# Nineteen differences per head for queries and keys, and the sums of key features times values taken head by head

## The chip, the cores and the metric

The kernel runs on one core of one Trainium2 chip. The metric is the time of one execution on the device in microseconds (us). Before the change the median of three runs is 1411.07 us (1410.63 to 1412.09).

Five engines work side by side, each through its own queue of instructions: TensorE (PE; its weight loads are a row of their own, PEld), VectorE (DVE), ScalarE (ACT), GpSimd (POOL) and SyncE (SP), which here issues the DMAs.

## What is computed

Two layers, each a linear attention with a learned feature map followed by a dense block, on 2048 rows of 640 numbers. Cut to what the change touches:

```
qkv = layernorm(x) @ wqkv                     # 32 heads of 20
pq, pk = q @ w_phi[h], k @ w_phi[h]           # per head, 20 by 20
phi = concat(softmax(p), softmax(-p))         # 40 features per head
kv  = sum over rows of phi_k * v              # per head 40 x 20
z   = sum over rows of phi_k                  # per head 40
o   = (phi_q @ kv) / (phi_q @ z + 1e-6)
x   = x + o @ wo
x   = x + mish(layernorm(x) @ w1 + b1) @ w2
```

A softmax over 20 numbers does not change when one and the same number is taken from all 20. So `p[d] - p[0]` serves as well as `p[d]`, and its first entry is always 0.

## The kernel before, in words

**Rows and blocks.** The 2048 rows are 16 tiles of 128 rows; two tiles are a block (8 blocks). A product in almost full precision is made of three matmuls on `fp32r` numbers, with both sides split into a high and a low part: high times high, high times low, low times high. So one projection of one tile to 640 columns is 2 halves of 320 columns x 5 parts of the inner dimension x 3 = 30 matmuls (`project`, `project_half`, line 344). Where the tables say `128x320`, that is the output of one of them. A plain `f32` matmul (transposes, the sums below, the averages) appears in the profile as two MATMUL instructions.

**The feature weights** are folded once, in layer 0: `fold_phi` (line 237) multiplies the weights of queries and of keys by the block-diagonal `phi_bd` (6 heads of 20 columns to a block, 120 columns to a matmul), splits the product into high and low part (ACT line 242, DVE line 243), and `spill_qk_weights` stores them in `wp_d` for layer 1.

**attend_first** goes over the 8 blocks. Per tile it projects keys, values and queries (`project`), and makes features of keys and queries (`features`): ACT copies the 640 numbers out of PSUM to every second group of 20 of a tile `e` of 1280 columns; DVE finds each head's maximum and minimum (368); DVE or POOL (369) and DVE (371) take them off; ACT takes the exponential of all 1280 (374, through the helper at 116); DVE sums each group (377) and inverts (378); POOL multiplies (379). Values go to a tile `v` of 21 columns per head, the last one 1, so that `z` comes out with `kv`. Then `keys` accumulates over the rows (line 414): for each of 11 groups of three heads (the last of two) one f32 matmul with the 63 columns of `v` as weights and the 120 features of the group as moving columns. Even groups write PSUM partitions 0 to 63, odd groups 64 to 127, of the tiles `kva` (groups 0 to 7) and `kvz` (8 to 10). Query features are turned by DVE (423) and stored in HBM (`e_d`).

**The passage.** All products of a group, also those of one head's features with another head's values, are in the sums. `finish_kv` clears the foreign ones by a multiplication with `head_mask` (three DVE products, 535), turns the result on PE (six transposes, 543) and copies it to `kvb` (ACT, DVE 547 and 548). The last query projection is spread around it: `rest()` issues its first half ahead of the last sums, and three fifths and two fifths of its second half before and after the transposes.

**attend_second** reads the query features back, multiplies them by `kvb` (`average`, line 571), divides (DVE 580 to 584) and applies `wo` (line 344 again). **dense** follows (lines 679 and 721).

**Order.** In `attend_second` and in the start of layer 0 the order of PE and SP (at the start of SP alone) is the one written down (`manual_schedule`); elsewhere a scheduler puts the instructions of each engine in order when the program is built. Every ACT instruction made by `act` comes after the one made before it. PSUM has two tiles `mm` of two banks each and four tiles `one` of one bank each.

Of the kernel before, what the change touches and what calls it, by code (L numbers as in the profile page):

```python
# [29 lines left out]
HC = D // 2  # L30
EW = 2 * D
# [7 lines left out]
E_CAP = 65536.0  # L39


@with_exitstack
def kernel(
# [48 lines left out]
    mask = const.tile([P, 120], F32, name="mask")  # L92

    kvb = const.tile([120, GP, P], F32, name="kvb")
# [4 lines left out]
    wp_d = dram.tile([2, 2, KD, P, D], F32, name="wp_d")  # L99
# [75 lines left out]
    def load_q_weights():  # L175
        ws = [r2_pair(k) for k in range(KD)]
        for k in range(KD):
            for s in range(2):
                nc.sync.dma_start(ws[k][s].bitcast(F32), wp_d[0, s, k])
        return ws  # L180

    def load_k_weights(kv_ws):
        for k in range(KD):
            for s in range(2):
                nc.sync.dma_start(kv_ws[k][s][:, :D].bitcast(F32), wp_d[1, s, k])

    def spill_qk_weights(kv_ws, q_ws):
        for k in range(KD):
            for s in range(2):
                nc.sync.dma_start(wp_d[1, s, k], kv_ws[k][s][:, :D].bitcast(F32))  # L190
                nc.sync.dma_start(wp_d[0, s, k], q_ws[k][s].bitcast(F32))
# [34 lines left out]

    def fold_phi(ws, bd, raw):

        pss = {}
        for k, c in ((0, 0), (1, 0), (2, 0), (3, 0), (0, 1), (1, 1), (2, 1), (3, 1), (4, 0), (4, 1)):  # L230
# [4 lines left out]
            for t in range(3 * c, 3 * c + 3):  # L235
                r, rows = raw[t]
                nc.tensor.matmul(ps[:, (t % 3) * 120:(t % 3) * 120 + rows],
                                 r[:rows, k * P:(k + 1) * P], bd[:rows, t, :rows],
                                 start=True, stop=True)
            n0, n1 = (0, 360) if c == 0 else (360, D)  # L240
# [88 lines left out]
    def project(xts, t, ws, col, ps=None):  # L329
# [4 lines left out]
        for c in range(2):  # L334
            project_half(ps[c], xts, t, ws, col, c)
        return ps

    def project_half(ps, xts, t, ws, col, c, ks=range(KD)):
        sl = slice(t * P, (t + 1) * P)
        cs = slice(col + c * HC, col + (c + 1) * HC)  # L340
        for k in ks:
            h, l, wh, wl = xts.hs[k], xts.ls[k], ws[k][0][:, cs], ws[k][1][:, cs]
            for n, (a, r) in enumerate(((h, wh), (h, wl), (l, wh))):
                nc.tensor.matmul(ps[:, :HC], a[:, sl], r, start=(k == 0 and n == 0),  # L344
                                 stop=(k == KD - 1 and n == 2))

    def both(ps):

        return ps[2][:, :, :HC]


# [3 lines left out]
    def features(ps, e, pool_sub):  # L355
# [3 lines left out]
        ec = e.rearrange("p (c h s d) -> p s c h d", c=2, s=2, d=DH)[:, 1]  # L359
        if len(ps) > 2:  # L360
            act(ec, both(ps).rearrange("p c (h d) -> p c h d", d=DH), AF.Copy)
        else:
            for c in range(2):
                act(ec[:, c], ps[c][:, :HC].rearrange("p (h d) -> p h d", d=DH), AF.Copy)
# [22 lines left out]
    def attend_first(layer, x_src, first):  # L387
# [18 lines left out]
        def keys(xts, i, v):  # L406
            e = big_tile()
            yield from features(project(xts, i % BT, kv_ws, 0), e, False)
            yield
            for g in range(G):  # L410
                p, n = divmod(g, 2)
                w, m = (120, 64) if g < 10 else (80, 42)
                acc, c = (kva, 120 * p) if p < 4 else (kvz, 120 * (p - 4))
                nc.tensor.matmul(acc[64 * n:64 * n + m, c:c + w], v[:, GW * g:GW * g + m],  # L414
                                 e[:, 120 * g:120 * g + w],
                                 start=(i == 0 and p in (0, 4)), stop=(i == NT - 1),
                                 skip_group_check=True)

        def queries(xts, i, ps=None):
            e = query_tile(i)  # L420
            yield from features(project(xts, i % BT, q_ws, 0) if ps is None else ps, e, True)
# [23 lines left out]
        if first is None:  # L445
            with tc.manual_schedule(engines={mybir.EngineType.SP}):
                bd = big_tile()[:120, :720].rearrange("p (t c) -> p t c", t=6)
                nc.sync.dma_start(bd[:, :3], phi_bd[:, :3])
                raw = load_raw(0, range(3))
                xt = fetch_normed(0)  # L450
                nc.sync.dma_start(bd[:, 3:], phi_bd[:, 3:])
                raw += load_raw(0, range(3, 6))
                nxt = normed(0, xt).all()
# [4 lines left out]
            nc.sync.dma_start(mask, head_mask)  # L458
# [3 lines left out]
        for b in range(NB):  # L462
# [9 lines left out]
            for n, (kind, t) in enumerate(order):  # L472
# [5 lines left out]
                if b == 0 and n == 3:  # L478
                    if layer == 0:
                        fold_phi(kv_ws, bd, raw)  # L480
                    kva, kvz = one_tile(), one_tile()
# [19 lines left out]
        def rest():  # L501

            ps = [one_tile(), one_tile()]
            project_half(ps[0], xts, 1, q_ws, 0, 0)
# [3 lines left out]
            project_half(ps[1], xts, 1, q_ws, 0, 1, range(3))  # L508
            yield
            project_half(ps[1], xts, 1, q_ws, 0, 1, range(3, KD))  # L510
# [6 lines left out]
        return kva, kvz, o_ws, loaded, rest()  # L517
# [12 lines left out]
    def finish_kv(kva, kvz, mask):  # L530
# [349 lines left out]
```

## Time and profile before

| | before |
|---|---|
| median of 3 runs | 1411.07 us |
| profiled execution, first to last instruction | 1410.6 us |
| PE busy | 1391.5 us (99%), 11528 matmuls |
| DVE busy | 1077.9 us (76%) |
| ACT busy | 583.6 us (41%) |
| POOL busy | 460.6 us (33%) |
| attend_first, layer 0 | up to about 274 us |
| attend_first, layer 1 | about 783 to 959 us |

The profile is of one execution. The span runs from its first to its last instruction; the table's 1410.6 us is the profiled execution's own time as the profile has it, and the median of the runs lies 0.5 us above. Matmuls are pipelined: one matmul's busy time is longer than the distance to the start of the next, so what a matmul costs is read from the distance between starts, not from its busy time. A group's row gives line, engine, operation, output and inputs, shapes, count, busy time, mean duration and the idle time ahead of it. In the chain of waits a piece is a stretch of equal instructions with its start and length.

### The profile page before, as it was taken

The numbers are of one execution on the slowest core, as the hardware profiler recorded it, in microseconds if no ns is written. First come the engines' busy times: TensorE is split into PE (matmuls) and PEld (weight loads), VectorE is DVE, ScalarE is ACT, GpSimd is POOL, SyncE is SP. The second block draws the span as 40 slices with busy tenths as digits, with TensorE's granted clock in tenths as the row PEclk, the third lists the DMA queues.
The fourth block names the chain that finished last, engine by engine and source line by source line (L and its number), as shares of the span: only waits on it lengthen the run. The fifth ranks groups of instructions, "written<-read, shape, count | busy, mean of one in ns | idle before, by whom it ended". The sixth has DMA issues, their size and how long they took to land. (4 is left out here: it accounts for less than half of the span.)

```text
span 1410.6 us, 28124 instructions
## 1 busy us (share of the span) xinstructions
PE 1391.5 (99%) x11528; PEld 1369.5 (97%) x11528; DVE 1077.9 (76%) x1810; ACT 583.6 (41%) x973; POOL 460.6 (33%) x344
## 2 busy tenths in 40 slices
PE   7999999999999999999999999999999999999998
PEld 7999999999999999999999999999999999999998
DVE  4798877686688877788769887878767766767765
ACT  4444343321355554455454333332234444444443
POOL 1354444343442221222234443443434211111112
PEclk9999999999999999999999999999999999999999
DMA  8533422789633423343374333357966212333200
GB/s 315 169 78 57 75 38 39 198 231 298 220 100 94 101 77 63 98 113 94 105 270 87 73 65 67 49 113 225 293 229 206 56 31 83 94 94 94 65 30 20
DMA packets 350035, 169.57 MB, mean 120 GB/s; under 512 B 286866, under 2 KB 323458, under 8 KB 349906
## 3 DMA queue, kind: packets, MB, share of 16 engines
q1 hardware_dynamic: 349906, 167.78, 44.1%
q8 instruction: 90, 1.47, 0.4%
q14 instruction: 39, 0.32, 0.1%
HBM read 104.82 MB, written 62.91 MB: 119 GB/s over the span
## 5 line engine op out<-in xcount | busy, mean ns | idle before, releaser
L721 PE MATMUL mm<-r2h,ol 128*128 128x320 f32 x1280 | 305.5, 310 | 1.4 <-ACT ol L704 0.8
L705 POOL TENSOR_TENSOR ol<-big,ol 128x512 fp32r<-128x512 f32 (+1 forms) x98 | 130.0, 1327 | 457.4 <-ACT ol L704 386.8
L679 PE MATMUL one<-xtl,r1h 128*128 128x256 f32 x960 | 268.6, 280 | 2.0 <-DVE xtl L286 2.0
L679 PE MATMUL one<-xth,r1l 128*128 128x256 f32 x960 | 268.0, 279 | 0.0
L679 PE MATMUL one<-xth,r1h 128*128 128x256 f32 x960 | 266.5, 279 | 0.0
L721 PEld LDWEIGHTS mm<-r2h,ol 128*128 128x128 f32 x1280 | 219.1, 188 | 3.1 <-POOL ol L705 1.8
L721 PE MATMUL mm<-r2l,ol 128*128 128x320 f32 x640 | 197.3, 309 | 0.0
L344 PE MATMUL mm<-r1h,xth 128*128 128x320 f32 x600 | 188.3, 314 | 0.0
L344 PE MATMUL mm<-r1h,xtl 128*128 128x320 f32 x600 | 185.7, 310 | 0.7 <-DVE xtl L286 0.7
L344 PE MATMUL mm<-r1l,xth 128*128 128x320 f32 x600 | 185.6, 309 | 0.0
L679 PEld LDWEIGHTS one<-xtl,r1h 128*128 128x128 f32 x960 | 180.4, 188 | 2.7 <-DVE xtl L286 2.5
L679 PEld LDWEIGHTS one<-xth,r1l 128*128 128x128 f32 x960 | 180.4, 188 | 0.0
L679 PEld LDWEIGHTS one<-xth,r1h 128*128 128x128 f32 x960 | 179.9, 188 | 0.0
L344 PE MATMUL mm<-r2h,xth 128*128 128x320 f32 x460 | 144.4, 314 | 0.0
L694 DVE TENSOR_SCALAR big<-big 128x512 f32<-128x512 f32 (+1 forms) x98 | 55.8, 570 | 113.4 <-ACT big L692 111.3
L344 PE MATMUL mm<-r2h,xtl 128*128 128x320 f32 x460 | 142.4, 310 | 0.0
L344 PE MATMUL mm<-r2l,xth 128*128 128x320 f32 x460 | 142.3, 309 | 0.0
L379 POOL TENSOR_TENSOR r<-r,r 128x1280 f32<-128x1280 f32 x32 | 75.7, 2367 | 144.5 <-DVE r L378 138.9
L692 ACT ACTIVATE big<-one,b1s 128x256 f32<-128x256 f32 x192 | 80.8, 469 | 96.0 <-PE one L679 93.8
L721 PEld LDWEIGHTS mm<-r2l,ol 128*128 128x128 f32 x640 | 120.2, 188 | 0.0
L696 ACT ACTIVATE big<-big,two 128x512 f32<-128x512 f32 (+1 forms) x98 | 70.1, 715 | 118.7 <-DVE big L695 116.2
L704 ACT ACTIVATE ol<-big 128x512 fp32r<-128x512 f32 (+1 forms) x98 | 61.0, 622 | 133.6 <-DVE big L703 133.3
(128 smaller groups left out, 3088.2 us busy)
## 6 DMA issues: line engine op xcount, KB each, us to landing
e_d<-r SPq DMA_DIRECT2D x128, 160.0 KB, 4.0
big<-e_d SPq DMA_DIRECT2D x32, 640.0 KB, 7.2
x_d<-xt SPq DMA_DIRECT2D x23, 640.0 KB, 4.1
xt<-x_d SPq DMA_DIRECT2D x22, 640.0 KB, 5.4
n_d<-xn SPq DMA_DIRECT2D x176, 80.0 KB, 2.1
xt<-in_x SPq DMA_DIRECT2D x16, 640.0 KB, 6.7
xn<-x_d SPq DMA_DIRECT2D x28, 320.0 KB, 4.3
v<-n_d SPq DMA_DIRECT2D x30, 256.0 KB, 3.1
```

The costliest lines, as they stand in the source:

```text
L344: nc.tensor.matmul(ps[:, :HC], a[:, sl], r, start=(k == 0 and n == 0), stop=(k == KD - 1 and n == 2))
L379: nc.gpsimd.tensor_tensor(eg, eg, r.unsqueeze(2).to_broadcast([P, 2 * H, DH]), op=ALU.mult)
L679: nc.tensor.matmul(ph[:, j, :], l, r, start=(n == 0), stop=(n == 3 * KD - 1))
L692: exps[0] = nc.scalar.activation(part(ta, 0)[:, j - js.start], ph[:, j, :], AF.Exp, bias=b1s[:, 2 * pr + j:2 * pr + j + 1]).ins
L694: nc.vector.tensor_scalar_min(e, e, E_CAP)
L696: nc.scalar.activation(r, n, AF.Ln, bias=two)
L704: nc.scalar.activation(ah[:, js], n, AF.Copy)
L705: nc.gpsimd.tensor_tensor(al[:, js], n, ah[:, js].bitcast(F32), op=ALU.subtract)
L721: nc.tensor.matmul(pys[t][:, c, :HC], l[:, j, sl], r, start=(f == 0 and n == 0), stop=(f == KF - 1 and n == 2))
```

## The change

It has two parts, and what follows from them.

**Differences.** At the start of layer 0 a new function `differences` takes the first column of each head from its other 19 in `bd`, the block-diagonal feature weights (two DVE instructions). `fold_phi` uses the 19 differences alone, so the folded weights of queries and keys are 608 columns wide in place of 640, and a projection's half is 304 columns in place of 320. Values and `wo` keep 320. `features` writes the 19 numbers behind a zero, which an added ACT instruction sets for all 32 heads of each tile. All later steps see 20 numbers per head, as before.

**Sums head by head.** `keys` issues 32 f32 matmuls per tile, one for each head, with 21 columns of `v` as weights and 40 moving columns. Four successive ones write four different quarters of 32 PSUM partitions (`HEAD_ORDER`, `head_place`). All sums fit one PSUM tile, and `kvz` is gone.

**The passage.** `finish_kv` has one clearing of a 360-column tile on POOL, four copies out of PSUM (one for each quarter, in turn on ACT and DVE), three transposes, and four DVE products with a mask that spread each head's block into `kvb`. The mask is loaded as 120 x 3 numbers. `average` reads `kvb` by group and not by pairs of groups.

```diff
+DF = DH - 1
+FC = H * DF // 2
+FW = H * DF
+HEAD_ORDER = [3 * (4 * n + q) + j for n in range(3) for j in range(3) for q in range(4) if 3 * (4 * n + q) + j < H]
...
-    mask = const.tile([P, 120], F32, name="mask")
-    kvb = const.tile([120, GP, P], F32, name="kvb")
+    mask = const.tile([120, 3], F32, name="mask")
+    kvb = const.tile([120, GP, 2, 64], F32, name="kvb").rearrange("f p q c -> f (p q) c")
...
+    def differences(bd, ts):
+        part = bd[:, ts].rearrange("p t (h d) -> p (t h) d", d=DH)
+        nc.vector.tensor_tensor(part[:, :, 1:], part[:, :, 1:],
+                                part[:, :, :1].to_broadcast([120, 18, DF]), op=ALU.subtract)
...
-                nc.tensor.matmul(ps[:, (t % 3) * 120:(t % 3) * 120 + rows],
-                                 r[:rows, k * P:(k + 1) * P], bd[:rows, t, :rows],
+                n, c0 = rows // DH, (t % 3) * 6 * DF
+                nc.tensor.matmul(ps[:, c0:c0 + n * DF].rearrange("p (h d) -> p h d", d=DF),
+                                 r[:rows, k * P:(k + 1) * P],
+                                 bd[:rows, t].rearrange("p (h d) -> p h d", d=DH)[:, :n, 1:],
...
-    def project_half(ps, xts, t, ws, col, c, ks=range(KD)):
+    def project_half(ps, xts, t, ws, col, c, ks=range(KD), w=HC):
-        cs = slice(col + c * HC, col + (c + 1) * HC)
+        cs = slice(col + c * w, col + (c + 1) * w)
-                nc.tensor.matmul(ps[:, :HC], a[:, sl], r, start=(k == 0 and n == 0),
+                nc.tensor.matmul(ps[:, :w], a[:, sl], r, start=(k == 0 and n == 0),
...
+    def head_place(h):
+        g, j = divmod(h, 3)
+        return g % 4, 2 * DH * (3 * (g // 4) + j)
...
+        act(eh[:, 1, :, 0], ident[:, :H], AF.Copy, scale=0.0)
-            act(ec, both(ps).rearrange("p c (h d) -> p c h d", d=DH), AF.Copy)
+            act(ec[..., 1:], both(ps, FC).rearrange("p c (h d) -> p c h d", d=DF), AF.Copy)
...
-            for g in range(G):
-                p, n = divmod(g, 2)
-                w, m = (120, 64) if g < 10 else (80, 42)
-                acc, c = (kva, 120 * p) if p < 4 else (kvz, 120 * (p - 4))
-                nc.tensor.matmul(acc[64 * n:64 * n + m, c:c + w], v[:, GW * g:GW * g + m],
-                                 e[:, 120 * g:120 * g + w],
+            for h in HEAD_ORDER:
+                q, c = head_place(h)
+                nc.tensor.matmul(kva[32 * q:32 * q + DH + 1, c:c + 2 * DH], v[:, (DH + 1) * h:(DH + 1) * (h + 1)],
+                                 e[:, 2 * DH * h:2 * DH * (h + 1)], start=(i == 0 and c == 0), stop=(i == NT - 1),
...
-    def finish_kv(kva, kvz, mask):
+    def finish_kv(kva):
+        acc = row_tile()
+        nc.gpsimd.memset(acc[:, :360], 0.0)
+        yield
+        for q, n in enumerate((9, 9, 8, 6)):
+            part = (slice(32 * q, 32 * q + DH + 1), slice(0, 40 * n))
+            if q % 2:
+                nc.vector.tensor_copy(acc[part], kva[part])
+            else:
+                act(acc[part], kva[part], AF.Copy)
+        yield
+        ps = one_tile().rearrange("p (n q c) -> p n q c", n=4, c=32)
+        for n in range(3):
+            nc.tensor.transpose(ps[:120, n], acc[:, 120 * n:120 * (n + 1)], ident)
+        for n, q, r, w in ((0, 4, 120, 3), (1, 4, 120, 3), (2, 2, 120, 3), (2, 1, 80, 2)):
...
+            nc.vector.tensor_tensor(
+                kvb[:r, g:g + q, :(DH + 1) * w].rearrange("f q (j c) -> f q j c", j=w),
+                ps[:r, n, q0:q0 + q, :DH + 1].unsqueeze(2).to_broadcast([r, q, w, DH + 1]),
+                mask[:r, :w].unsqueeze(1).unsqueeze(3).to_broadcast([r, q, w, DH + 1]), op=ALU.mult)
...
-                        kvb[:n, g // 2, 64 * (g % 2):64 * (g % 2) + w], start=True, stop=True)
+                        kvb[:n, g, :w], start=True, stop=True)
```

More of the change, by code (lines that the diff above doesn't have):

```diff
@@ L420, in queries @@
             e = query_tile(i)
[L421 removed]
+            yield from features(project(xts, i % BT, q_ws, 0, w=FC) if ps is None else ps, e, True)
             nc.vector.transpose(e, e)
@@ L609, in attend_second @@
         with tc.manual_schedule(engines={mybir.EngineType.PE, mybir.EngineType.SP}):
-            kv = finish_kv(kva, kvz, mask)
+            kv = finish_kv(kva)
+            next(kv)
             next(rest)
```

59 lines of the change are left out of this document (24 added, 35 removed).

## The prediction

> **What bounds the kernel now.** First the head of the page, then its slices: PE is busy for 99% of the span at the full clock, and DVE is the next engine.
>
> ```profile
> span 1410.6 us, 28124 instructions
> PE 1391.5 (99%) x11528; PEld 1369.5 (97%) x11528; DVE 1077.9 (76%) x1810; ACT 583.6 (41%) x973; POOL 460.6 (33%) x344
> PEclk9999999999999999999999999999999999999999
> ```
>
> A busy PE isn't a bound by itself, so next the chain of waits, in order of time, in the middle of layer 1's attend_first:
>
> ```profile
> 839.51 13.40 PE mm L344 x90
> 852.91 1.31 PE one L414 x22
> 854.22 13.40 PE mm L344 x90
> ```
>
> Nothing but PE is in it. One tile takes 854.22 - 839.51 = 14.71 us: 90 matmuls of the three projections and 22 instructions of the sums (11 f32 matmuls, two instructions each). So here the matmuls' own price decides, and both parts of the change touch just these two groups.
>
> What does a matmul cost by its width? The same chain in the dense block, where two widths follow each other:
>
> ```profile
> 1160.06 3.50 PE one L679 x30
> 1163.56 3.53 PE mm L721 x24
> ```
>
> 256 columns take 3.50/30 = 116.7 ns from start to start, 320 columns 3.53/24 = 147.1 ns. The price goes with the columns (0.456 and 0.460 ns each).
>
> **The change part by part.**
>
> *Projections.* Keys and queries have 2 layers x 16 tiles x 60 = 1920 matmuls. 304 columns at 0.46 ns cost 139.7 ns, so each saves 7.35 ns (7.6 by the slope between the two rows, 6.7 if a sixteenth of it did not follow the width). 30 matmuls per layer stand at the passage, treated below; the other 1860 save **13.7 us** (12.4 to 14.1).
>
> *Sums.* The timeline has a burst for one tile in layer 0 (195.45), the burst for two tiles at layer 1's passage (953.57), and, for the price of full width, the f32 matmuls of fold_phi:
>
> ```profile
> 195.21 0.31 PE L344 MATMUL mm<-r2h,xtl 128*128 128x320 f32 x1
> 195.45 1.38 PE L414 MATMUL one<-big,v 128*64 128x120 f32 x22
> 196.76 0.66 PE L280 MATMUL one<-ident,xn 128*128 128x128 f32 x4
> ...
> 953.57 2.54 PE L414 MATMUL one<-big,v 128*64 128x120 f32 x44
> 956.04 0.41 PE L344 MATMUL one<-r2h,xth 128*128 128x320 f32 x1
> ...
> 36.34 0.82 PE L237 MATMUL mm<-big,raw 120*128 120x120 f32 x6
> 37.01 0.83 PE L237 MATMUL one<-big,raw 120*128 120x120 f32 x6
> ```
>
> One tile: 196.76 - 195.45 = 1.31 us. Two tiles: 956.04 - 953.57 = 2.47 us. So the second costs 1.16 us: that is the stream of 22 instructions, 53 ns each, and 0.15 us is paid once per burst (with 0.09 us ahead of it: 0.24 from the last matmul's start to the burst's, where 0.147 is usual). At full output width 120 columns cost 0.67/6 = 112 ns. 53 is about half: the two halves of 64 output partitions work side by side.
>
> The new stream has 64 instructions of 40 columns, on four quarters. By the full-width price one costs 112/3 = 37 ns in its quarter. The fullest quarter has 9 heads, 18 instructions: 0.67 us if the four go side by side as the two do now. I take 0.68, since the weight loads get shorter too:
>
> ```profile
> L414 PEld LDWEIGHTS one<-big,v 128*64 128x64 f32 x640 | 32.7, 136 | 6.7 <-issue 5.6 <-POOL big L379 1.1
> L414 PEld LDWEIGHTS one<-big,v 128*42 128x42 f32 x64 | 7.1, 118 | 0.0
> ```
>
> The fixed part stays, since the burst's count and place do. But the number of instructions goes from 22 to 64 (and as many loads), and no row shows four quarters. The nearest rows in width are those of the averages, 42 and 63 columns on two halves:
>
> ```profile
> 959.35 1.38 PE L571 MATMUL mm<-kvb,big 120*64 120x63 f32 x40
> 960.57 0.27 PE L571 MATMUL mm<-kvb,ol 80*64 80x42 f32 x4
> 960.66 1.36 PE L571 MATMUL mm<-kvb,big 120*64 120x63 f32 x40
> ```
>
> 63 columns: (960.57 - 959.35)/40 = 30.5 ns, 42 columns: 0.09/4 = 22 ns. They give the dear end: 64 x 22 = 1.41 us, or 64 x 30.5 = 1.95 us. The cheap end is 0.60 us (18 x 33, the columns' price without any gap). These go with the columns too (0.48 and 0.54 ns a column, two at once), so I take the four side by side: the stream falls by 1.16 - 0.68 = 0.48 us for each of the 30 tiles outside the passages, **14.4 us** (16.8 at the cheap end; 7.5 or 23.7 us lost at the dear ones).
>
> The page "TensorEngine Tiling (Array Packing)" of the Trainium skill ("Performance Considerations") names a four-way column tiling for 32 output columns, which speaks for 0.68 us. The same section says that each matmul has an overhead of about 60 cycles, so that one column takes as long as 60; that speaks against the change, and no row here has four quarters to decide it.
>
> *The passage.* Around the end of layer 1's attend_first, on ACT, DVE and PE:
>
> ```profile
> 951.48 0.71 ACT L116 ACTIVATE r<-mm 128x640 f32<-128x640 f32 x1 [2.53 <-PE mm L344]
> 954.86 0.82 DVE L371 TENSOR_TENSOR r<-m,r 128x640 f32<-128x640 f32 x1 [1.09 <-POOL r L369]
> 955.72 1.28 ACT L116 ACTIVATE r<-r 128x1280 f32<-128x1280 f32 x1 [3.52 <-DVE r L371]
> 955.82 0.99 DVE L535 TENSOR_TENSOR xn<-one,mask 128x480 f32<-128x480 f32 x3
> 957.47 0.87 PE L543 MATMUL one<-ident,xn 128*120 128x128 f32 x6
> 958.11 0.60 ACT L116 ACTIVATE kvb<-one 120x512 f32<-120x512 f32 x1 [1.11 <-PE one L543]
> L116 ACT ACTIVATE r<-one 128x320 f32<-128x320 f32 x2 | 0.9, 436 | 0.4 <-PE one L344 0.4
> L584 DVE TENSOR_TENSOR xn<-mm,den 128x480 f32<-128x480 f32 x3 | 2.0, 657 | 0.1
> L584 DVE TENSOR_TENSOR xn<-mm,den 128x160 f32<-128x160 f32 x2 | 0.6, 311 | 0.0
> ```
>
> Now DVE alone takes the sums out, and PE reaches the transposes (957.47) and the averages (959.35) without a pause. After the change ACT takes two of the four copies, and ACT's instructions stay in order: behind the exponential that ends at 955.72 + 1.28 = 957.00. In the changed program as built each copy also waits for the one before it, since all use one tile. Copies of 360, 360, 320, 240 columns, in turn on ACT and DVE: ACT 0.46 (from 0.436 for 320), DVE 0.53 (657 - 311 over 320 columns is 1.08 ns each, and 0.14 fixed), 0.43, 0.40, with four hand-overs of 0.04 (955.68 to 955.72): 957.00 + 1.82 + 0.16 = 958.98. Meanwhile PE, faster by up to 1 us in the last two sums, stands idle, so their saving and that of the 30 matmuls here cover nothing. Three transposes need about 0.4 us, then six matmuls of 0.14 and a change of kind of 0.24: the averages start at 960.45. DVE's first two products (252 columns, 0.41 each) are ready by 960.3 (958.98 + 0.53 until the transposes have landed, where four needed 0.64 up to 958.11, + 0.82), the others before their groups' turn. 960.45 against 959.35 is 1.1 us per layer; layer 0's passage has the same layout. **+2.2 us** (0 if the copies ran side by side, +4 if the products were late too).
>
> *DVE in layer 0.* Where the sums get shorter PE asks DVE for features sooner:
>
> ```profile
> 60.00:100.00 40.00, 40.00 (x317) 38.88 (x318) 40.00 (x48) 18.14 (x26) 23.56 (x14) 1.00 0.37 69
> 840.00:940.00 100.00, 100.00 (x755) 98.19 (x754) 81.78 (x94) 34.42 (x50) 41.40 (x21) 1.00 0.38 64
> 87.22 2.76 POOL L379 TENSOR_TENSOR big<-big,r 128x1280 f32<-128x1280 f32 x1 [4.05 <-DVE r L378]
> 90.91 0.84 PE L414 MATMUL one<-big,v 128*64 128x120 f32 x12
> ```
>
> From 60 to 100 us DVE never stops (the busy figures after the stretch's length are PE, PEld, DVE, ACT, POOL). The features for the sums at 90.91 are ready at 89.98: 0.93 us to spare. PE would come there some 2.3 us earlier (two bursts, 0.96; some 180 matmuls of keys and queries, 1.3). **+1.4 us** is lost (0 to 2.6, all that PE gains in these 40 us). Later DVE has room: 81.78% of 14.71 is 12.0 us per tile against a new period of 13.8.
>
> *The small rest.* The differences cost DVE about 0.51 us each (342 columns by the slope above) on the way to the first two groups of fold_phi, whose next groups wait for DMAs anyway: +0.4 us (0 to 1.5). fold_phi's 200 instructions get 5% narrower, 112 to 106 ns: -0.5 us, since a good half stands where PE never waits. The added ACT instruction (0.26 us by the like one on values) stands right ahead of a copy out of PSUM for which ACT waits 2.53 us in the row above: hidden; without cover it would be 0.26 us on 64 tiles' latency, which no projection waits for. POOL's clearing is put early by the scheduler. Stores of the folded weights get 5% shorter off the path.
>
> **The sum**, against the profiled execution: 1410.6 - 13.7 - 14.4 + 2.2 + 1.4 + 0.4 - 0.5 = 1386.0 us. The median of the runs stands 0.5 us above that execution: **1386.5 us**, 1.7% faster.
>
> **The rivals.**
>
> *Two quarters at a time, or a queue that can't feed 128 instructions so fast* (0.20). For: only pairs are seen so far, and the 42-column row gives 22 ns. Then the stream takes 64 x 37/2 = 1.19 to 1.41 us: 0.9 to 7.5 us lost in place of 14.4 won. With less lost in layer 0: about 1401 to 1407, say 1403.
>
> *The price is per instruction* (0.11; the other side). If each small matmul with its load takes what 63 columns take, 30.5 ns, the sums take 1.95 us: +23.7 us, and 1411 - 13.7 + 23.7 + 2.2 = 1423 us. It decides above 1.55 us per tile (1.16 + 11.7/30), 24 ns per instruction. Against it: 42 columns took 22 ns on only two halves.
>
> *A floor under each start* (0.05), whatever quarter it goes to, a little above the 22 ns of the 42-column row: 23 to 27 ns make 1.47 to 1.73 us, 9 to 17 us lost, 1409 to 1417, say 1413. This is the rule of 60 cycles; the page "TensorE: Matmul & The Clock Gate" of the Trainium skill ("Wait — 56ns, not 53.3ns?") has a floor of about 25 ns from start to start. The 22 ns row lies below that, if over two halves.
>
> *Narrower projections save nothing* (0.04), as the weight loads, busy 188 ns each, would set the pace. Against: 256 columns with equal loads go at 117 ns. It gives 1400.
>
> ```profile
> L679 PEld LDWEIGHTS one<-xth,r1l 128*128 128x128 f32 x960 | 180.4, 188 | 0.0
> ```
>
> *DVE or the passages take more back* (0.06): 4 to 8 us, 1392.
>
> **The numbers.** Forecast 0.54, with 1381 to 1391 as its own range. The range 1380.5 to 1406 takes in the first rival, the last two and the unknown costs' bounds, and leaves out the two slow ones. 0.2% is about what a measurement of this kernel can tell from no change. Faster by more: 0.54 + 0.04 + 0.06 + 0.18 of the first rival = 0.82. Within: 0.02 of it and 0.03 of the floor: 0.05. Slower: 0.13.
>
> **What would show it.** In the chain, a tile's period of 13.8 us, of it 60 matmuls at 140 ns and 30 at 147. In the timeline, bursts of 64 that take 0.8 us up to the next start (1.3 to 1.6 for the first rival, over 1.7 for the second). At the passages, transposes that start 2 us after PE's last matmul, released by DVE. In the windows, PE below 40.00 of 40 in layer 0's second tile pair. Wrong from the start would be the forecast if the 304-column matmuls started 147 ns apart.

## The result and the profile after

The changed kernel takes **1398.26 us** (median of 4 runs, 1396.85 to 1400.08) against 1411.58 us before (4 runs, 1410.63 to 1412.49): a ratio of 0.9901 (0.9886 to 0.9916), 1.0% faster, where 1386.5 us and 1.7% were forecast. The time is 11.8 us above the forecast, outside the forecast's own range (1381 to 1391). It lies in the wider range of 1380.5 to 1406, but that was stretched so far for the rival of two quarters at a time, which the bursts below refute: there the range held by luck.

The head of the page after:

```profile
span 1395.7 us, 30855 instructions
PE 1364.8 (98%) x12866; PEld 1344.2 (96%) x12866; DVE 1080.8 (77%) x1814; ACT 592.4 (42%) x1039; POOL 466.4 (33%) x346
```

The timeline of PE after, first in the middle of layer 1, then at the bursts that divide the program:

```profile
856.78 0.30 PE L358 MATMUL mm<-r2l,xth 128*128 128x304 f32 x1
856.92 0.30 PE L358 MATMUL mm<-r2h,xtl 128*128 128x304 f32 x1
857.15 0.83 PE L432 MATMUL one<-big,v 128*21 128x40 f32 x64
857.91 0.41 PE L358 MATMUL mm<-r1h,xth 128*128 128x304 f32 x1
...
870.91 0.83 PE L432 MATMUL one<-big,v 128*21 128x40 f32 x64
...
102.66 0.83 PE L432 MATMUL one<-big,v 128*21 128x40 f32 x64
260.66 1.48 PE L432 MATMUL one<-big,v 128*21 128x40 f32 x128
802.15 0.83 PE L432 MATMUL one<-big,v 128*21 128x40 f32 x64
937.57 1.48 PE L432 MATMUL one<-big,v 128*21 128x40 f32 x128
```

304 columns cost 140 ns from start to start (856.78 to 856.92). A burst takes 857.91 - 857.15 = 0.76 us up to the next start, against 1.31 us before; one tile takes 870.91 - 857.15 = 13.76 us against 14.71. So in the steady part both savings are there. The same four bursts before (the last one, 953.57, stands in the prediction):

```profile
99.61 1.38 PE L414 MATMUL one<-big,v 128*64 128x120 f32 x22
268.89 2.54 PE L414 MATMUL one<-big,v 128*64 128x120 f32 x44
808.73 1.38 PE L414 MATMUL one<-big,v 128*64 128x120 f32 x22
```

They cut the span into five stretches. "Forecast" is what the prediction's terms give for each: 0.48 us saved for every burst of one tile, 0.00735 us for every matmul of 304 columns outside the passages, both counted in the trace, and its other terms where it put them.

| stretch, us | before | after | difference | forecast |
|---|---|---|---|---|
| start to the sums of tile 4, layer 0 | 99.6 | 102.7 | +3.1 | -2.2 |
| to the last two tiles' sums, layer 0 | 169.3 | 158.0 | -11.3 | -10.1 |
| to the sums of tile 5, layer 1 | 539.8 | 541.5 | +1.7 | -3.5 |
| to the last two tiles' sums, layer 1 | 144.8 | 135.4 | -9.4 | -9.0 |
| to the end of the span | 457.0 | 458.1 | +1.1 | +1.1 |

(Tiles are counted from 1. The column adds up to -23.7 and not to the prediction's -24.6, because the prediction counted 30 tiles outside the passages. There are 28: the last two tiles of each layer share the burst at the passage.) The second and fourth stretch came out better than forecast, by 1.2 and 0.4 us, and the fifth as forecast. The loss is in two places: the start of layer 0 (5.3 us) and from layer 0's passage to the start of layer 1 (5.2 us). What PE waited for, from the list of its waits, before (first fence) and after:

```profile
PE one L414 <- POOL big L379: 0.9, 1, 0.9
```

```profile
PE mm L358 <- ACT r L122: 6.6, 2, 3.5
...
PE one L564 <- DVE xn L558: 5.3, 2, 2.7
```

The columns are us in total, times, longest. The waits for loads and for the feature weights in the first 20 us are left out (8.3 us before, 8.7 after). New are two waits for the copy of a query projection out of PSUM (`r`, 6.6 us), one in each layer's start, and two for the copies at the passages (5.3 us). (The list counts idle time; the expectations below count from start to start, 0.3 us more for each wait.)

How the first one comes about, in the timeline of layer 0 after:

```profile
78.80 1.60 DVE L264 BATCH_NORM_STATS2 bn<-xt 128x6 f32<-128x320 f32 x4
80.33 1.52 DVE L388 TENSOR_REDUCE m<-big 128x32 f32<-128x640 f32 x2
81.77 1.50 DVE L440 STREAM_TRANSPOSE r<-r 128x1280 f32<-128x1280 f32 x1
83.30 3.54 SPq L444 DMA_DIRECT2D e_d<-r  x4
89.90 0.26 ACT L122 ACTIVATE r<-ident 128x32 f32<-128x32 f32 x1 [9.69 <-DMA e_d<-r]
...
90.75 0.41 PE L358 MATMUL mm<-r1h,xth 128*128 128x304 f32 x1 [3.48 <-ACT r L122]
```

Read it from the end. PE waits 3.48 us for a free `mm`. ACT would empty it, but stands for 9.69 us until the store of the query features two tiles back has freed their buffer; the store starts at 83.30, behind DVE's turn of those features at 81.77. Before, that turn came at 77.33, ahead of the block statistics (`bn`) and of the next tile's maxima:

```profile
77.33 1.50 DVE L423 STREAM_TRANSPOSE r<-r 128x1280 f32<-128x1280 f32 x1
```

So DVE's instructions have another order, though only some of them changed.

A second new thing stands in the windows. The columns are the stretch, its length, the busy time of PE, PEld, DVE, ACT, POOL, the granted clock, the DMA share and GB/s:

```profile
88.50:91.90 3.40, 1.15 (x8) 1.16 (x9) 3.40 (x5) 2.00 (x4) 2.75 (x1) 1.00 0.26 52
...
91.90:95.30 3.40, 3.40 (x73) 2.99 (x72) 3.37 (x6) 1.09 (x4) 3.15 (x2) 0.50 0.00 0
262.60:266.00 3.40, 0.99 (x8) 0.74 (x6) 1.22 (x3) 2.27 (x4) 0.00 (x0) 1.00 0.83 275
266.00:269.40 3.40, 3.14 (x23) 2.84 (x25) 1.25 (x5) 0.89 (x3) 0.00 (x0) 0.50 1.00 390
...
938.40:941.80 3.40, 2.10 (x71) 1.79 (x59) 0.96 (x2) 1.62 (x2) 0.72 (x1) 1.00 0.53 163
941.80:945.20 3.40, 2.04 (x33) 1.86 (x35) 1.85 (x6) 1.54 (x4) 0.00 (x0) 1.00 0.97 339
```

Behind three of the four waits (that at 754 us is the third) PE runs for 3.4 us at half clock, up to 1.7 us of work lost each time. The page's slices, 35 us wide, don't show it (all nines). Behind the fourth, PE's wait for the copies in layer 1, which is as long as the one in layer 0 (2.7 us), there is none: an edge between two stretches splits it, and PE is busy for 2.1 and 2.0 us of the two.

### The profile page after: what moved, and what is told of

It reads as the page before. It is cut to its first block, busy times and chain, and to the rows that moved or that the text cites. A ratio compares the mean times of both kernels' runs of the same rounds, so it can differ in the third digit from the quotient of the medians.

```text
span 1395.7 us, 30855 instructions
## 1 busy us (share of the span) xinstructions
PE 1364.8 (98%) x12866; PEld 1344.2 (96%) x12866; DVE 1080.8 (77%) x1814; ACT 592.4 (42%) x1039; POOL 466.4 (33%) x346
## 5 line engine op out<-in xcount | busy, mean ns | idle before, releaser
L358 PE MATMUL mm<-r1h,xth 128*128 128x304 f32 (+1 forms) x600 | 187.5, 313 | 6.6 <-ACT r L122 6.6
L358 PE MATMUL mm<-r1h,xtl 128*128 128x304 f32 (+1 forms) x600 | 184.7, 308 | 1.0 <-DVE xtl L300 1.0
L358 PE MATMUL mm<-r1l,xth 128*128 128x304 f32 (+1 forms) x600 | 184.4, 307 | 0.0
L358 PE MATMUL mm<-r2h,xth 128*128 128x304 f32 (+1 forms) x460 | 142.2, 309 | 0.0
L358 PE MATMUL mm<-r2h,xtl 128*128 128x304 f32 (+1 forms) x460 | 140.4, 305 | 0.0
L358 PE MATMUL mm<-r2l,xth 128*128 128x304 f32 (+1 forms) x460 | 140.3, 305 | 0.0
L358 PEld LDWEIGHTS mm<-r1h,xth 128*128 128x128 f32 x600 | 113.8, 190 | 8.1 <-ACT r L122 7.0
```

The lines of the kernel that those rows point to most:

```text
L358: nc.tensor.matmul(ps[:, :w], a[:, sl], r, start=(k == 0 and n == 0), stop=(k == KD - 1 and n == 2))
```

## The experiments

The theory after the first look: PE saves what was forecast; four waits and three stretches at half clock take about half of it back. Against it stood: the clock falls on account of the new small matmuls; only one part of the change pays; DVE's throughput, not a buffer or an order, makes the waits.

Ratios are to the kernel before on the same chip, with their 95% intervals.

### The differences alone

```diff
-            for h in HEAD_ORDER:
-                q, c = head_place(h)
...
+            for g in range(G):
+                p, n = divmod(g, 2)
...
-    def finish_kv(kva):
+    def finish_kv(kva, kvz, mask):
```

(the sums and the passage as before, 304-column projections kept)

> The differences alone: keys and queries with 304 columns, sums in pairs of 120 columns and the passage as before. My theory (the matmuls save what was forecast, and four waits of PE take about half of it back: one in each passage and one at the start of each layer's query tiles): the 304-column matmuls start 140 ns apart, the sums take 1.16 us per tile, PE waits under 1 us in each passage, and the granted clock stays 1.0 there. Projections -13.7 us, fold and differences about 0, so 1398 us if the waits at the layers' starts belong to the sums, and up to 1405 if they come with the narrower projections and the added ACT instruction. First rival (the lower clock comes with the new kind of small matmuls on quarters, not with PE's waits): no stretch at half clock anywhere in this kernel, whatever its waits. Second rival (only one part pays, and this one doesn't): 1411.

1405.73 us, 0.9951 (0.9937 to 0.9966). The passages have no wait, but the two waits for `r` are there, 5.0 us together, and half clock behind both:

```profile
87.00:90.40 3.40, 1.14 (x8) 0.88 (x7) 3.40 (x4) 1.59 (x3) 2.65 (x1) 1.00 0.32 59
90.40:93.80 3.40, 3.40 (x21) 3.10 (x21) 3.40 (x7) 1.50 (x5) 2.71 (x3) 0.51 0.00 0
```

This kernel has no matmul on quarters, so the first rival falls: half clock comes without them, behind waits. The waits at the layers' starts belong to the differences, and they cost this part half of its 13.7 us.

### The sums alone

```diff
-DF = DH - 1
...
-                differences(bd, slice(0, 3))
...
-        act(eh[:, 1, :, 0], ident[:, :H], AF.Copy, scale=0.0)
```

(640-column weights, 320-column projections, the new sums and the new passage)

> The sums on quarters and the new passage alone, projections at 320 columns and no differences. My theory: a burst of 64 takes about 0.75 us up to the next start, -14 us over 30 tiles and some 1 us more in the passages; against that each passage waits about 3 us for the four chained copies (+2.5 each), and one or more stretches of 3.4 us at half clock behind these waits cost 1.7 each: 1411.6 - 15 + 5 + 2 to 3 = 1403 to 1405 us. First rival (the lower clock comes with the new small matmuls and not with the waits): stretches at half clock also where PE has not waited. Second rival (the waits at the layers' starts belong to the sums alone): 3.8 and 2.5 us of wait there as in the whole change, and 1409 us.

1401.36 us, 0.9920 (0.9904 to 0.9937), better than expected. PE waits 4.6 us for the copies at the passages, but no stretch at half clock follows (mean clock 1.000), and the layers' starts have no wait for `r` (1.9 us for POOL's products and 1.7 us for `xtl` in all). In layer 0 the order of DVE's instructions is that of the kernel before from the first turn of query features (60 us) up to 109 us. Both parts pay, 6.7 and 11.1 us; together they should give 17.8 and give 13.3.

### One copy in place of four

```diff
+                    nc.tensor.matmul(kva[:, :360], ident, zero.to_broadcast([P, 360]), start=True, stop=False, skip_group_check=True)
...
-        for q, n in enumerate((9, 9, 8, 6)):
...
-                act(acc[part], kva[part], AF.Copy)
+        nc.vector.tensor_copy(acc[:, :360], kva[:, :360])
```

> The whole change, but the bank of the sums is cleared ahead by one matmul over all 128 partitions, so that one DVE copy of 360 columns takes the sums out in place of the four chained ones on ACT and DVE; POOL's clearing goes too. My theory: the transposes no longer wait for ACT's exponential; PE's wait at each passage falls from 2.97 us to under 1 us, the half-clock stretch at 266 us is gone, and the time falls by 2 x 2.3 + 1.7 = 6 us to about 1392 us; the waits at the layers' starts stay (3.8 and 3.3 us), each with its half-clock stretch. Rival (the clock falls on account of the new matmuls): the stretch at 266 us stays though the wait is gone, and the time is 1393.5 to 1394. Rival (the passage's wait is that for DVE's products and not for the copies): under 2 us gained, 1396 to 1398.

1392.48 us, 0.9856 (0.9842 to 0.9871), as the theory had it. At layer 0's passage (timeline; before the edit the averages start 268.60 - 260.66 = 7.94 us behind the burst):

```profile
261.79 1.48 PE L434 MATMUL one<-big,v 128*21 128x40 f32 x128
264.70 0.54 PE L561 MATMUL one<-ident,xn 128*120 128x128 f32 x3
266.01 1.38 PE L591 MATMUL mm<-kvb,big 120*64 120x63 f32 x40
```

Here it is 4.22 us. The transposes wait for nothing, and the half clock at 266 us is gone. The waits for `r` stay (6.7 us), with half clock behind both. From layer 0's passage to the sums of tile 5 in layer 1 (799.70) this kernel takes 537.9 us, 3.6 us less than the change as made.

### A third buffer for query features

```diff
-        return r2_wide(10 + i % 2, F32).rearrange("p s d -> p (s d)")
+        if i % 3 == 2:
+            return big_tile()
+        return r2_wide(10 + i % 3, F32).rearrange("p s d -> p (s d)")
```

> The whole change with a third buffer for the query features, so that the evacuation of a query tile's projection no longer waits for the store of the query tile two before it. My theory: PE's waits of 3.79 us in layer 0 (at 87 us) and 3.34 + 1.32 us in layer 1 (at 754 us) fall to what they were before the change (0 and 2.2 us) with their two half-clock stretches, and the time falls by 3.8 + 2.5 + 2 x 1.7 = 9.7 us at most to 1389 us, 1392 if DVE, busy without a pause there, still holds PE up by some 2 us. Rival (DVE's throughput in layer 0 sets PE's wait and not the buffer): the wait at 87 us moves to the next tile and stays about 3 us; under 4 us gained in all, from layer 1. Rival (the added ACT instruction sets it): nothing gained, 1398.

1399.78 us, 0.9911 (0.9896 to 0.9926): nothing gained. The wait for `r` is gone from the list, and others stand in its place:

```profile
PE one L434 <- POOL big L401: 3.9, 2, 2.0
PE mm L358 <- ACT xth L122: 2.6, 2, 1.5
```

My theory of the buffer falls. With the buffer's wait gone, features and copies that follow late instructions of DVE end last: layer 0's waits fall from 3.5 to 1.8 us, but those at layer 1's start rise from 4.1 to 5.4. There is also more half clock: 6.8 us at the start of layer 1, and 3.4 us behind layer 1's passage, whose wait of 2.7 us is as long as in the changed kernel. Here it fell almost whole into one stretch (941.56 to 944.98, PE busy for 1.19 us).

### The heads in their own order

```diff
-HEAD_ORDER = [3 * (4 * n + q) + j for n in range(3) for j in range(3) for q in range(4) if 3 * (4 * n + q) + j < H]
+HEAD_ORDER = list(range(H))
```

> The whole change with the heads of the sums taken in their own order, so that three heads in a row (six instructions) go to the same quarter of 32 output partitions, where the change goes round the quarters. What tells: the time of a burst of 64 from its start to the next start, 0.75 us in the whole change. If each quarter has a queue of its own, it stays at about 0.75 us. If instructions start strictly in order and one waits for the end of the one before it in its quarter, three of four quarters stand idle most of the time: 32 heads x 2 x 37 ns less the overlap at the changes of quarter, 1.6 to 2.0 us per burst, 26 to 38 us more in all (about 1430 us). Between these, if a few instructions can pass a waiting one.

1408.07 us (one run). The burst in the middle of layer 1:

```profile
835.94 1.22 PE L432 MATMUL one<-big,v 128*21 128x40 f32 x64
837.09 0.41 PE L358 MATMUL mm<-r1h,xth 128*128 128x304 f32 x1
```

1.15 us, between the two cases: instructions for one quarter do hold up those behind them, but not fully. Going round the quarters is worth 0.39 us of the 0.55 us per tile.

### PE kept busy at the passage

```diff
+        for _ in range(11):
+            nc.tensor.matmul(ps[:, :P], ident, ident, start=True, stop=True, skip_group_check=True)
```

(ahead of the transposes, into their tile)

> The whole change with 11 f32 matmuls of the identity by itself (128 columns, 22 instructions, 2.4 us by 0.11 us each) ahead of the transposes of each passage, so that PE is busy while it waits for the copies; their results are overwritten. Theory (a stretch at half clock follows where PE has stood idle for most of a stretch of 3.4 us): the passage still lasts as long, but the half-clock stretch at 266 us is gone, 1.7 us less; those at 92 and 757 us stay. Rival (the clock falls for another reason, such as the small matmuls): the stretch at 266 us stays.

1396.61 us (one run). In this run a stretch at half clock begins at 754.74 us; counted back from it in steps of 3.413 us, these are the stretches at the first passage and around the wait in layer 0's start, which lasts 3.5 us here too:

```profile
263.22:266.63 3.41, 3.21 (x36) 2.84 (x37) 1.99 (x6) 1.57 (x5) 0.00 (x0) 1.00 1.06 390
...
85.73:89.14 3.41, 1.56 (x11) 1.30 (x9) 3.41 (x6) 0.00 (x0) 1.75 (x4) 1.00 0.89 140
89.14:92.55 3.41, 1.73 (x12) 1.73 (x13) 3.41 (x5) 2.58 (x6) 2.72 (x2) 1.00 0.11 28
```

With useless work in the wait the clock stays, as the theory had it, but this run alone doesn't show why. PE comes to the passage 1.4 us earlier than in the changed kernel, so without the filler (262.04 to 264.66) the edge at 263.22 would have split the idle time: an estimate from the timeline is PE busy for 2.4 and 1.8 us of the two stretches, and in none of these runs does the clock fall behind that much work. That half clock comes from idling, and not from the small matmuls, is shown by the runs together: the differences alone have half clock without small matmuls, the sums alone and the last kernel below have small matmuls without half clock, and the clock falls only behind stretches in which PE was idle for over half the time (last section). Two parts of the expectation missed. There is no half clock near 92 us, though PE waits as long as in the changed kernel: there the wait fell into one stretch (PE busy for 1.15), here over two (1.56 and 1.73). And at the start of layer 1 half clock lasts 6.8 us, twice as long as expected.

### 320 columns in the first block of each layer

```diff
-            yield from features(project(xts, i % BT, kv_ws, 0, w=FC), e, False)
+            yield from features(project(xts, i % BT, kv_ws, 0, w=FC, x=16 if i < 2 else 0), e, False)
...
+                nc.gpsimd.memset(half[:, FW:D].bitcast(F32), 0.0)
```

> The whole change, but in the first block of each layer the projections of keys and queries are again 320 columns wide (16 zero columns each that nobody reads; the stored weights are 640 wide again). That makes PE 240 x 7.35 ns = 1.8 us slower, and the scheduler, which puts DVE's instructions in order by times that it reckons, comes back to nearly the order of before: query features turned ahead of the next tile's statistics and maxima. Theory now (the third buffer gained nothing, so what makes PE wait at the layers' starts is the new order of DVE's instructions, not a lack of buffers nor the amount of work): the waits at 87 us (3.79) and 754 us (3.34 + 0.43 + 1.32) fall to those of before (0 and 2.2) with their half-clock stretches: -3.8 - 2.9 - 3.4 + 1.8 = -8.3 us, about 1390 us. Rival (DVE has too much work there for the faster PE, in whatever order): the waits stay within 1 us of what they were and the time is 1398 to 1400.

1400.64 us, 0.9918 (0.9904 to 0.9933): the time speaks for the rival, the trace less so. The wait at 87 us is gone, where DVE's order is that of before; behind the place where it still differs there are new ones, 1.68 us for `xth` at 91 and 2.29 us for `xtl` at 95 us:

```profile
91.93 0.82 DVE L394 TENSOR_TENSOR r<-m,r 128x640 f32<-128x640 f32 x1 [0.70 <-POOL r L392]
93.62 2.38 DVE L279 SCALAR_TENSOR_TENSOR stats<-mv,stats 128x1 f32<-128x1 f32 x2 [0.86 <-POOL stats L277]
...
97.32 0.41 DVE L303 TENSOR_TENSOR xtl<-one,xth 128x256 fp32r<-128x256 f32 x1
```

DVE waits twice for POOL, in order, and the 0.41 us for `xtl` that PE needs stand behind it all. So the wait moved along with the part of the order that was still new, and layer 0 gained nothing. At layer 1's start the waits fell from 4.1 to 2.5 us, but a stretch at half clock (774.9) is still there, and layer 1's passage has one now (945.6).

### The same with one copy

```diff
+        nc.vector.tensor_copy(acc[:, :360], kva[:, :360])
...
+            yield from features(project(xts, i % BT, kv_ws, 0, w=FC, x=16 if i < 2 else 0), e, False)
```

> The kernel with one copy in place of four and, with it, the 320-column projections in the first block of each layer. By the theory that the order of DVE's instructions makes the waits at the layers' starts: 1392.5 - 3.7 - 3 - 3.4 + 1.8, about 1384 us, and no half-clock stretch left, which is what the prediction forecast for the change. By the rival that DVE's work itself sets these waits: 1392 to 1394.

1394.21 us, 0.9869 (0.9853 to 0.9885): no better than one copy alone, as the rival had it. PE waits 5.5 us for `xtl` and 1.7 us for `xth`: 4.0 us of it in layer 0, much as just seen, and the rest at layer 1's start. Half clock is left at one place (100.2).

### The zeroing on POOL

```diff
-        act(eh[:, 1, :, 0], ident[:, :H], AF.Copy, scale=0.0)
+        nc.gpsimd.memset(eh[:, 1, :, 0], 0.0)
```

> As the kernel with 320-column projections in the first block of each layer, and with the zeroing of each head's first feature moved from ACT to POOL. In that kernel DVE's order was that of before only up to the second block of layer 0, and the wait moved there (1.88 us at 91 and 2.60 us at 95 us); with the zeroing on POOL the scheduler gives back DVE's whole order of before up to the third block, in both layers. Theory (the order of DVE's instructions makes the waits of layer 0, and two things set that order off: the narrower projections and the added ACT instruction): PE waits under 1 us in all between 70 and 120 us and the half-clock stretch at 99 us goes: -4 - 1.7 and no more, about 1394 to 1395 us. Rival (the work itself, in whatever order): waits of 4 to 5 us stay there, 1400 us. Rival (POOL, whose memsets now wait for stores of query features, holds up the features): the wait turns up on POOL, 1398 to 1405 us.

1398.70 us, 0.9910 (0.9895 to 0.9924). Both the theory and the third rival came true, at different places. From 84 to 98 us PE is now busy for 13.55 us (10.52 in the changed kernel), without half clock:

```profile
84.00:98.00 14.00, 13.55 (x209) 12.74 (x208) 14.00 (x21) 5.04 (x8) 10.33 (x10) 1.00 0.07 15
```

But at 120 us a new wait stands, and it begins on POOL:

```profile
115.48 0.16 POOL L382 MEMSET r<- 128x32 f32 x1 [1.67 <-DMA e_d<-r]
...
117.55 2.89 POOL L402 TENSOR_TENSOR big<-big,r 128x1280 f32<-128x1280 f32 x1 [0.84 <-DVE stats L279]
```

The passage also waits longer (3.78 us for the copies in layer 0), and half clock follows both passages (6.8 us from 264.8, 3.4 us from 944.1). The sum is no gain.

### The zeroing alone, in the kernel before

```diff
+        act(eh[:, 1, :, 0], ident[:, :H], AF.Copy, scale=0.0)
```

> The kernel before with one thing added: the ACT instruction that zeroes every head's first feature (its value is then overwritten by the copy out of PSUM). No differences, no new sums. As built, DVE's order in layer 0 changes from the second block on, to that of the kernel with 320-column projections in the first blocks. Theory (order): a wait of PE of 2 to 4 us between 85 and 100 us that the kernel before doesn't have, and a half-clock stretch behind it if it falls into one stretch of 3.4 us: +2 to +5 us, 1414 to 1417 us, though the instruction itself is 64 x 0.26 us on an engine that is busy for 41% of the time. Rival (only the faster PE makes the waits): no new wait, 1411 to 1413 us.

1413.47 us (10 runs, 1412.79 to 1414.25) against 1411.42: 1.0013 (1.0003 to 1.0023), slower, at the low end of what the theory gave. PE is no faster here, and still waits 1.39 us for `xtl` at 97 us. In this window DVE never stops, neither before (first line) nor now; but now ACT does nothing and PE waits:

```profile
94.00:98.00 4.00, 4.00 (x29) 4.00 (x28) 4.00 (x5) 2.03 (x3) 3.94 (x3) 1.00 0.06 8
...
94.00:98.00 4.00, 2.61 (x18) 2.34 (x18) 4.00 (x6) 0.00 (x0) 1.58 (x2) 1.00 0.01 4
```

The order of DVE's instructions is that of the kernel before up to 76.6 us, and another from there on. So the 0.26 us instruction doesn't cost by its time; that it costs by the order that DVE gets is the reading that fits both.

### All three edits

```diff
+        nc.gpsimd.memset(eh[:, 1, :, 0], 0.0)
...
+            yield from features(project(xts, i % BT, kv_ws, 0, w=FC, x=16 if i < 2 else 0), e, False)
...
+        nc.vector.tensor_copy(acc[:, :360], kva[:, :360])
```

> All three edits together: one copy in place of four at the passage, 320-column projections in the first block of each layer, zeroing on POOL. By the theory of the order: the kernel with the first two (1394.2 us, waits of 4.95 us between 70 and 120 us and one half-clock stretch) less 4 and 1.7 us, 1388 to 1389 us; below the kernel with one copy alone (1392.5). By the rival of the work: 1393 to 1395 us.

1391.89 us, 0.9862 (0.9847 to 0.9878), between the two: POOL's memsets again (PE waits 2.6 us for POOL's products).

### The zeroing on POOL in the first blocks alone

(against the kernel with all three edits)

```diff
-        nc.gpsimd.memset(eh[:, 1, :, 0], 0.0)
+        if early:
+            nc.gpsimd.memset(eh[:, 1, :, 0], 0.0)
+        else:
+            act(eh[:, 1, :, 0], ident[:, :H], AF.Copy, scale=0.0)
```

> As the kernel with all three edits, but the zeroing stands on POOL only for the first two blocks of each layer, where it gave DVE's order back, and on ACT elsewhere. In the kernel with all three edits PE still waits 1.85 and 1.78 us at 120 and 122 us and 1.34 us at 798 us; at 117 us a memset on POOL waits for the store of an earlier tile of query features and holds up POOL's statistics and products behind it. Theory (these waits come from the memsets on POOL, those at the start from DVE's order): they go, and the others stay away: 1391.9 - 3.6 - 1.3 = 1387 us, which is the forecast made for the change. Rival (some wait is left wherever DVE is busy without a pause, whoever zeroes): the waits turn up elsewhere, 1391 to 1393 us, like the kernel with one copy alone.

**1387.51 us** (5 runs, 1387.13 to 1388.06), 0.9828 (0.9815 to 0.9842): faster than the kernel before by 1.7% and than the change as made by 0.7%, as the theory had it. Its bursts:

```profile
99.98 0.83 PE L440 MATMUL one<-big,v 128*21 128x40 f32 x64
259.15 1.48 PE L440 MATMUL one<-big,v 128*21 128x40 f32 x128
794.51 0.83 PE L440 MATMUL one<-big,v 128*21 128x40 f32 x64
929.93 1.48 PE L440 MATMUL one<-big,v 128*21 128x40 f32 x128
```

The five stretches are 100.0, 159.2, 535.4, 135.4 and 455.8 us: against the change as made, 2.7 us are back at the start, 6.1 between the passage and layer 1's start and 2.3 in the last stretch, and 1.2 are lost in the second. No stretch at half clock is left ahead of the program's last microsecond.

## Why the prediction was right or wrong

**Projections, -13.7 us: right, a little too large.** 304 columns take 140 ns. In the steady part a tile saves 0.95 us, of which the sums save 0.55; that leaves 0.40 us for 60 matmuls, 6.7 ns each where 7.35 was taken, or 12.4 us in all. That is the low end of the prediction's range, which was itself worked out too low: if a sixteenth of 7.35 ns doesn't follow the width, 6.9 ns are left, or 12.8 us.

**Sums, -14.4 us: right in kind, too small for each tile, and counted for two tiles too many.** The four quarters run side by side: 0.55 us saved per tile where 0.48 was taken. Over the 28 tiles outside the passages that is 15.4 us, where 28 times 0.48 is 13.4 (the prediction's own cheap end for 28 tiles is 15.7). So the rivals of two quarters at a time, of a price per instruction and of a floor under each start all fall: 64 instructions (two for each of 32 matmuls) in 0.76 us are 12 ns each. The Trainium skill's page "TensorE: Matmul & The Clock Gate" ("Wait — 56ns, not 53.3ns?") has a floor of about 25 ns from start to start; here the measurement decides.

**The passage, +2.2 us: right.** In layer 1 the averages start 944.47 - 937.57 = 6.90 us behind the burst, before 959.35 - 953.57 = 5.78: +1.1 us, with the transposes released by DVE's copy, at the end of the chain that starts behind ACT's exponential (layer 0's shown, then layer 1's averages):

```profile
263.11 1.27 ACT L122 ACTIVATE r<-r 128x1280 f32<-128x1280 f32 x1 [3.75 <-DVE r L391]
...
266.26 0.90 PE L564 MATMUL one<-ident,xn 128*120 128x128 f32 x3 [2.67 <-DVE xn L558]
268.60 1.74 PE L594 MATMUL mm<-kvb,big 120*64 120x63 f32 x40
...
944.47 1.38 PE L594 MATMUL mm<-kvb,big 120*64 120x63 f32 x40
```

In layer 0 it is 268.60 - 260.66 = 7.94 us, another 1 us, which comes with the half clock from 266.00 on; no step of the prediction had that.

**DVE in layer 0, +1.4 us (0 to 2.6): this step failed.** It read rightly that DVE never stops between 60 and 100 us, and set the bound at "all that PE gains in these 40 us". The stretch lost 5.3 us against the forecast: a wait of 3.5 us for `r`, and half clock behind it. The step took DVE's instructions to keep their order, without giving a reason. They didn't: the narrower projections and the added ACT instruction each moved it, as the experiments show in pairs (with the order of before PE is busy for 13.55 of 14 us, the ACT instruction alone brings a wait, and the sums alone, which keep the order, have no wait for `r`). With the order of before the stretch takes 100.0 us in the last kernel, against 99.6 before the change: there all that PE gains is lost, which is the step's bound, and hardly more. The rival "DVE or the passages take more back" named this kind of loss, but with 4 to 8 us and a chance of 0.06.

**"Later DVE has room": this failed for the start of layer 1.** It was read from the steady part (81.78% busy). At the start of layer 1 the kernel before has a stretch that is nearly as full as layer 0's:

```profile
750.00:800.00 50.00, 48.38 (x378) 47.03 (x377) 47.46 (x48) 17.75 (x25) 23.39 (x12) 1.00 0.41 73
```

DVE is busy for 47.46 of 50 us. The stretch from layer 0's passage to here lost 5.2 us, layer 0's half clock at the passage among them.

**"The added ACT instruction ... hidden": wrong in kind.** Its time is hidden, as said. Even so the kernel before takes 2.0 us more with it (1.0013), and with it DVE's order is another.

**"The median of the runs stands 0.5 us above that execution".** The time of a run is 1.8 us more than its span (1397.5 and 1395.7 for the profiled one after the change). So the 0.5 us meant that the profiled execution before was slower than most (some 1412.4 us against a median of 1411.07); after the change it is 0.8 us faster than the median, which stands 2.6 us above its span. This makes 2.1 us of the miss. The count of two tiles too many makes 1.0, and the stretches 8.8 (5.3 and 5.2 lost in the first and third, 1.2 and 0.4 better in the second and fourth, 0.1 rounding): 11.8 us with rounding.

Of the 6.1 us that came back between the passage and layer 1's start, 3.6 come with one copy alone, which takes away the passage's wait and the half clock behind it. The other 2.5 come with the two edits that move DVE's order, and how they divide between the wait there and the half clock is open. DVE's order was only moved by edits that also move other things, never by itself, so that the order makes the waits is argued from pairs of kernels and not shown alone.

## What to carry to other kernels

Where an engine off the critical path is full in one stretch, a faster bottleneck engine gains nothing there (100.0 us against 99.6 here, with the old order); and if a scheduler orders the queues by times that it reckons, any edit, even one hidden instruction, can reorder that full queue and lose more than the edit saves. So compare the queue orders of the two programs in every stretch where a second engine is over 90% busy, not the steady part alone. And count a wait of about 3 us on PE as its length and, depending on where it falls, nothing, 1.7 us or up to 3.4 us more.

## What the runs showed of the hardware

Small f32 matmuls with 40 columns, going round four quarters of 32 output partitions, start every 12 ns on average (0.76 us for 64); with six in a row to the same quarter it is 18 ns (1.15 us).

PE's granted clock changes at the edges of stretches of 3.413 us that follow each other without a gap: in the changed kernel half clock begins at 91.92, 266.00 and 757.52 us, which are 51 and 144 times 3.413 us apart. Between the first 20 us and the last 20 us of all these runs it falls to a half 23 times. Each time PE was busy for 0.51 to 1.62 us of the stretch ahead; it never falls behind 1.71 us or more, and stayed once behind 1.56 us. The stretch with the most work ahead of a fall is at layer 1's passage of the kernel with the zeroing on POOL:

```profile
940.65:944.06 3.41, 1.62 (x19) 1.44 (x21) 1.98 (x6) 1.31 (x4) 0.00 (x0) 1.00 1.05 344
```

Half clock lasts 3.4 us, in three of the kernels once 6.8 us. What counts is where the wait falls: one of 3.5 us brought half clock in the changed kernel, an equally long one in the kernel with the filler none. The Trainium skill's page "TensorE: Matmul & The Clock Gate" ("What's actually happening") has a free-running window of about 3.4 us, with which the traces agree, and lets the clock fall after at least one idle window; here a window with PE busy for nearly half of it was enough.
